# The first block's scores placed in the feed-forward banks, with the front of the schedule planned again

## The chip, the cores and the metric

The kernel runs on one core of a Trainium2 chip. The metric is the device time of one execution in microseconds (us); a time quoted below is the median of several executions. PE is TensorE, ACT is ScalarE, DVE is VectorE, POOL is GpSimd, SP is SyncE. A "trace" is the record of one profiled execution.

## The reference, cut to what matters

Attention with eight global keys and a local window of 96, for 4 sequences of 768 tokens with 8 heads of 64; then a feed-forward layer with softplus over all 3072 tokens. Inputs and output are float32.

```python
scores = scale * np.matmul(q, k.transpose(0, 1, 3, 2))      # 4 x 8 x 768 x 768
keep = is_global | is_local                                 # 8 global keys, 96 local ones
scores = np.where(keep, scores - slopes * dist, -1e9)
a = softmax(scores)
x = np.matmul(a, v) ...                                     # -> 3072 x 512
h = x @ w_in                                                # 512 -> 2048
g = np.maximum(h, 0) + np.log1p(np.exp(-np.abs(h)))         # softplus
return g @ w_out                                            # 2048 -> 512
```

## The kernel before

The tokens are cut into 24 blocks of 128 (attention) and 12 groups of 256 (feed-forward). A block needs only the keys of itself and of the block before it. A built-in list scheduler orders all operations of all engines; each operation is given with a rank and an estimated duration, and some 200 hand-tuned constants (`NUDGE`) push single operations forward or back. So a program is a layout plus a set of constants that were tuned for this layout.

The pieces of PSUM that matter: two score tiles `s_ps` of two banks each, two feed-forward banks `h_ps`, one bank `o_ps` and one bank `x_ps`. A block's scores are 8 heads times 128 (first block of a sequence) or 256 (other blocks) columns. They are written in one or two groups of matmuls:

```python
def scores(n, parts, rank):                     # parts: (0, 1) at once where n is in WHOLE
    ...
    def seed():                                 # only for blocks in PE_BIAS
        for part in parts:
            for y in range(2):
                src = (biasA if i else bias0)[:, part, ...]
                nc.tensor.matmul(s_ps[s_of(n, part)][:, y, 0 : 256 * u_all], ident[:], src...,
                                 start=True, stop=False, skip_group_check=True)
    ...
    def fn():
        for part in parts:
            for m in range(2):
                for u in range(u_all):
                    for y in range(2):
                        rows = slice(64 * y, 64 * y + 64)       # 64 rows of the array: one head
                        nc.tensor.matmul(reg, kt[rows, 2 * part + m, :], qv(rows, 2 * part + m),
                                         start=not biased, stop=True, skip_group_check=biased)
```

`soften()` then adds the bias on DVE (into a float32 tile `z`) where PE did not seed it, and ACT takes the exponential into `pb`; `pv()` multiplies by the values. A feed-forward slot is `mm1` (eight matmuls of 256 columns from `w_in` into an `h_ps` bank), an `Exp` and, for two slots together, a `Ln` on ACT (softplus), and later `mm2` (matmuls of 512 columns with `w_out`). In the first 33 us, where data is still being loaded, PE is kept busy with matmuls on zeros that nobody reads:

```python
def filler(j):
    def fn():
        nc.tensor.matmul(x_ps[:, 0:256], blank[:, 0:P], blank[:, 0:256])
    return op(f"fill{j}", "PE", 0.11, 1e6 + j, fn, reads=["blank"])
...
FILLERS = 90
PE_BIAS = (0, 1, 3)
WHOLE = (0, 4, 6, 7, 8, 9, 10, 12, 13, 14, 15, 16, 17, 18, 23)
...
order = pl.run()
for o in order:
    o.ins = o.fn()                              # emission in the planned order
```

The softmax here doesn't subtract the row's maximum and nothing guards it: scores larger than these inputs give would overflow.

Of the kernel before, what the change touches and what calls it, by code (L numbers as in the profile page):

```python
# [23 lines left out]
class Planner:  # L24
# [54 lines left out]
    def run(self, first=0.7, dma_first=1.0, dma_last=1.4, fixed=None, stretch=None):  # L79
# [40 lines left out]
        while True:  # L120
# [50 lines left out]
            while events and events[0][0] <= now + 1e-9:  # L171
                _, _, kind, o = heapq.heappop(events)
                if kind == "free":
                    free[o.eng] = True
                    if o.work:
                        queues[o.eng].append([o, o.work * stretch(o), now + dma_first])
                    else:
                        o.end = now
                        tell([u for u in o.users if u.eng == o.eng])
                        push(now + o.lat, "done", o)  # L180
                else:
                    o.done = True
                    tell([u for u in o.users if o.work or u.eng != o.eng])
# [6 lines left out]
FIRST_LOADS = "v0 k0 q0 i3 i1 q1 o0 v1 k1 i0 i2 i7 i4 o1 i6 q2 k2 i5 o5 o2 o3 o7 v2 o6 o4".split()  # L190
LOAD_LEAD = 2.5
LEADS = {3: 2.25, 4: 2.75, 5: 3, 6: 2.75, 7: 2.75, 8: 3.5, 9: 2.25, 10: 2.75, 11: 3.5}
FILLERS = 90
TABLE_RANK = -9000.0
BIAS0_ON = ["ACT", "DVE"]
BIASA_ON = ["ACT"]
PE_BIAS = (0, 1, 3)
PE_KEYS = {
    0: (("s", 1, 0), ("s", 1, 1), ("h1",), ("o",)),
    1: (("s", 0, 0), ("s", 0, 1), ("s", 1, 0), ("s", 1, 1)),  # L200
    2: (("s", 1, 0), ("x",), ("s", 0, 0), ("s", 0, 1)),
}
PE_X = {0: ("h0",), 1: ("h0",), 2: ("o",), 3: ("o",), 4: ("x",), 5: ("x",)}
# [11 lines left out]
    (0, 0): ("s", 0, 0),  # L215
# [7 lines left out]
NARROW = (0,)  # L223
TAIL = 8.0
ENG = {
    0: {"k": ["POOL", "DVE"], "q": ["POOL", "ACT"], "tk": ["DVE", "ACT"], "tq": ["DVE", "DVE"], "v": ["POOL"]},
    1: {"k": ["DVE", "POOL"], "q": ["POOL", "DVE"], "tk": ["ACT", "DVE"], "tq": ["DVE", "DVE"], "v": ["POOL", "DVE"]},
    2: {"k": ["ACT", "DVE"], "q": ["POOL", "POOL"], "tk": ["DVE", "DVE"], "tq": ["DVE", "DVE"], "v": ["POOL", "ACT"]},
}
ENG_X = {0: "DVE", 1: "ACT", 2: "DVE", 3: "DVE", 4: "ACT", 5: "ACT"}  # L230
ENG_W = {
    "i0": "DVE",
    "i1": "POOL",
    "i2": "POOL",
    "i3": "DVE",
# [5 lines left out]
    "o1": "POOL",  # L241
# [10 lines left out]
    "a0.2": 2,  # L252
    "a0.5": 1,
    "a0.6": -1,
    "a0.7": 0.5,
    "a1.0": -2,
    "a1.1": -1,
    "a1.3": -2,
    "a1.4": -2,
    "a1.5": 4,  # L260
    "a1.6": 2,
# [4 lines left out]
    "b0.0.10": 0.5,  # L266
    "b0.0.14": 0.5,
    "b0.0.4": 0.5,
    "b0.0.6": -8,
    "b0.0.8": -1,  # L270
    "b0.1.0": 1,
    "b0.1.10": 1,
    "b0.1.12": 1,
    "b0.1.2": -8,
    "b0.1.8": -8,
    "b1.0.0": -0.5,
    "b1.0.10": -0.5,
    "b1.0.12": 1,
    "b1.0.14": 4,
    "b1.0.2": -1,  # L280
    "b1.0.6": -1,
# [6 lines left out]
    "biasFalse0": -1,  # L288
    "biasFalse1": -2,
    "biasFalse2": 0.5,  # L290
    "biasFalse3": -2,
    "biasFalse4": -2,
    "biasFalse5": 4,
    "biasFalse6": -4,
    "biasFalse7": -2,
    "biasTrue0": 1,
    "biasTrue1": -4,
    "biasTrue3": 2,
    "biasTrue4": 4,
    "biasTrue6": 0.5,  # L300
    "biasTrue7": 2,
    "castk0.1": -8,
    "castk1.0": 1,
    "castk1.1": 4,
    "castk2.0": 8,
    "castk2.1": 1,
    "castk3.00": -0.5,
    "castk3.10": -0.5,
    "castk4.00": 8,
    "castk4.01": -8,  # L310
    "castk4.11": 8,
    "castq0.0": 1,
    "castq0.1": 0.5,
    "castq1.1": -1,
    "castq2.0": -4,
    "castq2.1": 8,
    "castq4.0": 8,
    "castv0.00": -4,
    "castv0.11": -0.5,
    "castv1.00": -8,  # L320
    "castv1.01": 2,
    "castv1.11": -2,
    "castv2.00": 0.5,
    "castv2.01": -0.5,
    "castv2.10": 8,
    "castv2.11": -8,
    "castv3.11": -2,
# [5 lines left out]
    "cin2": -1,  # L333
    "cin3": 4,
    "cin4": -2,
    "cout0": -2,
    "cout1": 1,
    "cout3": -0.5,
    "cout5": -1,
    "cout6": -4,  # L340
    "cpk0.0": -1,
    "cpk0.1": 2,
    "cpk1.0": 0.5,
# [4 lines left out]
    "cpq2.0": 0.5,  # L348
    "cpq2.1": 8,
    "d0": 0.5,  # L350
    "d0e": 2,
    "dl0a": 2,
    "dl0b": 0.5,
    "dl0c": 8,
    "dl1a": 8,
    "dl1c": 8,
    "e0.1": 4,
    "e0.3": 2,
    "e0.5": 1,
    "e0.7": -8,  # L360
    "e1.0": -8,
    "e1.2": 8,
    "e1.4": -8,
    "e1.5": -1,
    "e1.6": -4,
    "e1.7": 4,
# [4 lines left out]
    "ex1.1": -1,  # L371
    "ex2.0": -2,
    "ex3.1": 8,
    "ex4.1": -1,
    "ex5.0": -0.5,
    "ex5.1": 1,
    "gk5": -8,
    "gk7": 0.5,
    "gv4.0": -0.5,
    "gv4.1": 8,  # L380
    "gv5.0": 1,
    "gv5.1": 2,
    "gv6.0": -8,
    "gv6.1": 4,
    "gv7.0": 2,
    "gv8.0": -8,
    "gv8.1": -0.5,
    "ldk0.0": 1,
    "ldk0.1": -1,
    "ldk1.0": 8,  # L390
    "ldk1.1": -0.5,
    "ldk2.0": 2,
    "ldk4": 8,
    "ldk5": 0.5,
    "ldq0.0": -0.5,
    "ldq0.1": 8,
    "ldq1.0": 2,
    "ldq2.0": 0.5,
    "ldq2.1": 2,
    "ldq3": -4,  # L400
    "ldv1": 8,
    "ldv2": 8,
# [4 lines left out]
    "ln0.0": -1,  # L407
    "ln0.1": 1,
    "ln0.3": -2,
    "ln1.0": 2,  # L410
    "ln1.1": 0.5,
    "ln1.3": -4,
    "nm0.0": -0.5,
    "nm0.1": -1,
    "nm1.0": -0.5,
    "nm2.1": -1,
    "nm3.0": 0.5,
    "nm4.0": 0.5,
    "nm4.1": -0.5,
    "nm5.0": -4,  # L420
    "nm5.1": 8,
    "nm6.0": 2,
    "nm6.1": 1,
    "oc0.0.0": 8,
    "oc0.1.0": -0.5,
    "oc1.0.0": 2,
    "ones": 4,
    "pv0.1": -8,
    "pv1.0": -8,
    "pv1.1": -1,  # L430
    "pv2.0": -2,
    "pv3.0": -1,
    "pv4.1": 8,
# [4 lines left out]
    "sb1.0": 1,  # L438
    "sb1.1": -0.5,
    "sb2.0": -2,  # L440
    "sb3.0": -2,
    "sb4.0": 1,
    "sb4.1": -4,
    "sc0.1": -4,
    "sc1.0": 8,
    "sc1.1": 0.5,
    "sc2.0": -0.5,
    "sc3.0": -8,
    "sc4.0": -0.5,
    "sc5.1": -1,  # L450
    "sc6.1": -4,
    "sc7.0": -0.5,
    "sc7.1": 4,
    "st0.0.0": 0.5,
    "st0.1.0": -1,
    "st1.0.0": -4,
    "table": -1,
    "trk0.0": -8,
    "trk2.0": 0.5,
    "trk2.1": 2,  # L460
    "trk3": 0.5,
    "trk4": -2,
    "trq0.0": -4,
    "trq1.0": -0.5,
    "trq1.1": -2,
    "trq2.0": 2,
    "trq3": -0.5,
    "trq4": 8,
    "win0": 8,
    "win1": 8,  # L470
    "win2": -1,
    "win3": -2,
    "win4": -2,
    "win5": 8,
    "win6": 0.5,
    "win7": -8,
    "wout0": 1,
    "wout3": -1,
    "wout4": 4,
    "wout5": 4,  # L480
    "wout6": 0.5,
    "wout7": 8,
    "xc0": 2,
    "xc1": 8,
    "xc2": -1,
    "xc3": -2,
    "xc4": -1,
    "xc5": -4,
    "xt1": -1,
    "xt2": 1,  # L490
    "xt3": 2,
    "xt4": 1,
    "xt5": 0.5,
    "z4.0": 1,
    "z4.1": 0.5,
# [4 lines left out]
DIST0_ON = "ACT"  # L500
S_ON = {
    (0, 0): 0,
    (0, 1): 1,
    (1, 0): 0,
    (1, 1): 1,
# [5 lines left out]
    (4, 1): 1,  # L511
# [3 lines left out]
    (6, 1): 1,  # L515
    (7, 0): 1,
    (7, 1): 0,
}
T0 = 11.0
LATER = 55.0  # L520
MARGIN = {-1: 10.5, 0: -15.0, 1: 69.0, 2: 65.5, 3: 21.0}
SOONER = {"cin": -20.0, "cout": -25.0}
LAST_KEYS = (("s", 0, 0), ("x",), ("o",))
WHOLE = (0, 4, 6, 7, 8, 9, 10, 12, 13, 14, 15, 16, 17, 18, 23)
LOAD_ON = {"q0": "ACT"}


@with_exitstack
def kernel(
# [11 lines left out]
    nc = tc.nc  # L541
# [110 lines left out]
    def raw_slot(name):  # L652
        raw_of[name] = len(raw_of) % NRAW
        return raw_of[name]
# [38 lines left out]
    def load_w(which, p, rank, eng):  # L693

        slot = raw_slot((which, p))
        half, c = p % 2, p // 2
        raw = raw_t[slot][:].rearrange("p (a c) -> p a c", a=2)
        cost, issue = (1.37, 86.0), 0.45
        if which == "in" and c in NARROW:
            raw = raw_t[slot][:].rearrange("p (a c) -> p a c", a=NM)  # L700
            src = moe_w_in[:, W * p : W * p + W]
            dst = w_in_bf[:, :, W * p : W * p + W]
            cost, issue = (1.51, 51.0), 1.05
        elif which == "in":
            src = moe_w_in[W * half : W * half + W, 512 * c : 512 * c + 512]
            dst = w_in_bf[:, 2 * half : 2 * half + 2, 512 * c : 512 * c + 512]
        else:
            src = moe_w_out[W * p : W * p + W, :]
            dst = w_out_bf[:, 2 * p : 2 * p + 2, :]
        op(f"w{which}{p}", "SP", issue, rank, lambda: nc.sync.dma_start(raw, src.rearrange("(a p) c -> p a c", p=P)),  # L710
           writes=raw_keys(slot), dma=cost)
        op(f"c{which}{p}", eng, t_copy(eng, 1024, True), rank, lambda: copy_on[eng](dst, raw),  # L712
           reads=raw_keys(slot), writes=[("w" + which, p)], port=eng == "DVE")
# [71 lines left out]
    def kt_of(n):  # L785
        return kt_unit(unit_of(n))[:, n % 2, :, :]
# [13 lines left out]
    def v_keys(n):  # L800
        return [("vb", vb_slot(n), r) for r in range(2)]
# [71 lines left out]

    def scores(n, parts, rank):
# [70 lines left out]
    def pv(n, part, key, rank):  # L945
        i = blocks[n][1]
        u_all = 2 if i else 1
        pb, xs = pb_t[(2 * n + part) % NPB], xs_t[n % NXS]
# [4 lines left out]
        def mm():  # L953
            for h in range(4):
                for u in range(u_all):
                    nc.tensor.matmul(  # L956
                        xv[:, h, :], pb[:, u_all * (2 * (h % 2) + h // 2) + u, :],
                        vb_of(prev if u else n)[:, 4 * part + h, :], start=u == 0, stop=u == u_all - 1,
                    )

        reads = [("pb", (2 * n + part) % NPB), "ones"] + v_keys(n) + (v_keys(prev) if i else [])
# [232 lines left out]
    def attend(n, rank):  # L1194
# [4 lines left out]
        for parts in ((0, 1),) if n in WHOLE else ((0,), (1,)):  # L1199
            scores(n, parts, rank + 0.1 * parts[0])  # L1200
            for part in parts:
                soften(n, part, rank + 0.1 * part)
# [137 lines left out]
```

## Time and profile before

| | before |
|---|---|
| median time | 222.69 us (222.26 to 223.04, 3 runs) |
| span in the trace | 219.9 us |
| PE / ACT / DVE / POOL busy | 97% / 73% / 50% / 42% |
| matmuls, of which fillers | 2062, 90 |

The page divides the span into 40 slices of 5.5 us; a digit is the busy share of a slice in tenths. These are the three rows that the argument uses:

```profile
PE   8999999999999999999999999999999999999994
...
ACT  5664979936889798678788688678689678887300
...
DMA  5999999999999797999993241999921222011112
```

PE is at 9 in every slice between the first and the last. In the front ACT reaches 9 in slices 5, 7 and 8, and the DMA engines are nearly full for the first half. A 9 for PE says nothing about what PE does: in slices 1 to 6 a large part are fillers.

### The profile page before, as it was taken

The page shows a single profiled execution, that of the slowest core. Times are in us where ns is not written, and L with a number is a line of the kernel's source. Part 1 is how long each engine was busy: PE and PEld are TensorE (multiplying, and loading weights), DVE is VectorE, ACT ScalarE, POOL GpSimd, SP SyncE. Part 2 cuts the span into 40 slices and gives each one's busy share as a digit, 9 for nine tenths or more (in the row PEclk, how much of TensorE's full clock was granted, in tenths as well). Part 3 has the DMA queues.
Part 4 walks back from the last instruction along what each step waited for, and adds up shares of the span by engine and source line. Part 5 has one row for each costly group of instructions (what it writes and reads, how often), then busy time and mean ns, then how long its engine had stood idle before and what let it go on. Part 6 is the DMA issues. An engine that isn't in the chain of part 4 may idle for free.

```text
span 219.9 us, 5042 instructions
## 1 busy us (share of the span) xinstructions
PE 213.5 (97%) x2034; PEld 150.1 (68%) x2062; DVE 109.5 (50%) x204; ACT 160.1 (73%) x216; POOL 91.6 (42%) x156
## 2 busy tenths in 40 slices
PE   8999999999999999999999999999999999999994
PEld 6787786656685876666757757766657777767554
DVE  6467465644676567338347348347548642001121
ACT  5664979936889798678788688678689678887300
POOL 4647776787551566804972403126702220000000
DMA  5999999999999797999993241999921222011112
GB/s 207 329 351 377 380 362 381 290 254 232 241 236 256 232 235 180 190 272 243 174 205 84 51 143 60 141 263 303 162 81 51 51 72 72 3 48 48 44 56 95
DMA packets 70359, 40.96 MB, mean 186 GB/s; under 512 B 30144, under 2 KB 62272, under 8 KB 70336
## 3 DMA queue, kind: packets, MB, share of 16 engines
q1 hardware_dynamic: 69904, 40.05, 71.9%
q10 hardware_dynamic: 432, 0.59, 0.8%
q8 instruction: 16, 0.26, 0.5%
q14 instruction: 7, 0.06, 0.1%
HBM read 27.26 MB, written 6.29 MB: 153 GB/s over the span
## 4 chain that ended last, share of the span: by engine, by line
PE 82%; DMA 10%; ACT 3%; SPq 3%; issue 1%; DVE 0%; ACTq 0%
PE h_ps L1013 35%; PE o_ps L1062 30%; PE s_ps L1062 5%; PE s_ps L906 5%; PE x_ps L956 5%; DMA raw<-in_moe_w_in_dram 4%; DMA raw<-in_k_dram 4%; DMA raw<-in_v_dram 2%; PE x_ps L1062 2%; SPq L710 2%; ACT e L1028 1%; ACT g L1039 1%; SPq L675 1%; ACT vb L754 1%; ACT kb L730 0%
## 5 line engine op out<-in xcount | busy, mean ns | idle before, releaser
L1013 PE MATMUL h_ps<-XT,w_in_bf 128*128 128x256 bf16 x768 | 95.9, 273 | 0.8 <-ACT e L1028 0.5
L1013 PEld LDWEIGHTS <-w_in_bf 128*128 128x128 bf16 x768 | 72.7, 98 | 18.1 <-issue 0.6
L1028 ACT ACTIVATE e<-h_ps 128x512 f32<-128x512 f32 x96 | 60.1, 631 | 31.6 <-PE h_ps L1013 31.3
L1062 PE MATMUL o_ps<-w_out_bf,g 128*128 128x512 bf16 (+1 forms) x296 | 74.1, 371 | 1.2
L1062 PEld LDWEIGHTS <-g 128*128 128x128 bf16 x416 | 37.5, 98 | 29.3
L932 DVE TENSOR_TENSOR z<-s_ps,biasA 128x1024 f32<-128x1024 f32 x36 | 43.3, 1219 | 17.9 <-PE s_ps L906 12.8
L1039 ACT ACTIVATE g<-e 128x1024 bf16<-128x1024 f32 x48 | 50.7, 1057 | 1.4
L939 ACT ACTIVATE pb<-z 128x1024 bf16<-128x1024 f32 (+1 forms) x42 | 41.1, 987 | 4.1 <-DVE z L932 4.0
L754 POOL CAST vb<-raw 64x512 bf16<-64x512 f32 x44 | 27.5, 624 | 14.9 <-DMA raw<-in_v_dram 13.2
L754 POOL CAST kb<-raw 64x512 bf16<-64x512 f32 x36 | 22.3, 620 | 25.9 <-DMA raw<-in_k_dram 24.6
L1091 DVE COPY osb<-o_ps 128x512 f32<-128x512 f32 (+1 forms) x20 | 13.4, 670 | 38.2 <-PE o_ps L1062 38.0
L863 POOL COPY vb<-vb 4x512 bf16<-4x512 bf16 x32 | 19.9, 621 | 29.6 <-PE x_ps L956 26.3
L956 PEld LDWEIGHTS <-pb 128*128 128x128 bf16 x352 | 16.6, 98 | 5.8
L966 DVE RECIPROCAL rcp<-x_ps 128x4 f32<-128x4 f32 x40 | 7.1, 179 | 23.5 <-PE x_ps L956 23.4
L967 DVE TENSOR_TENSOR xs<-x_ps,rcp 128x256 bf16<-128x256 f32 x40 | 17.0, 424 | 1.4
L956 PE MATMUL x_ps<-vb,pb 128*128 128x65 bf16 x304 | 15.9, 193 | 0.0
L1174 PE MATMUL x_ps<-blank 128*128 128x256 bf16 x90 | 12.9, 295 | 1.1 <-DVE blank L1113 1.1
L1062 PE MATMUL s_ps<-w_out_bf,g 128*128 128x512 bf16 (+1 forms) x62 | 13.1, 352 | 0.1
L906 PEld LDWEIGHTS <-kT 64*128 64x128 bf16 x224 | 6.8, 94 | 6.1 <-issue 5.7
L1174 PEld LDWEIGHTS <-blank 128*128 128x128 bf16 x90 | 9.0, 107 | 2.9 <-DVE blank L1113 1.0
L906 PE MATMUL s_ps<-qT,kT 64*128 64x128 bf16 x224 | 10.5, 218 | 0.0
L712 POOL CAST w_out_bf<-raw 128x1024 bf16<-128x1024 f32 x7 | 7.3, 1039 | 3.4 <-DMA raw<-in_moe_w_out_dram 3.4
(72 smaller groups left out, 102.9 us busy)
## 6 DMA issues: line engine op xcount, KB each, us to landing
raw<-in_v_dram SPq DMA_DIRECT2D x12, 512.0 KB, 5.2
out_dram<-osb SPq DMA_DIRECT2D x23, 256.0 KB, 2.8
raw<-in_q_dram SPq DMA_DIRECT2D x9, 512.0 KB, 5.4
raw<-in_k_dram SPq DMA_DIRECT2D x9, 512.0 KB, 5.8
raw<-in_moe_w_in_dram SPq DMA_DIRECT2D x8, 512.0 KB, 9.9
raw<-in_moe_w_out_dram SPq DMA_DIRECT2D x8, 512.0 KB, 9.3
raw<-in_k_dram SPq DMA_DIRECT2D x6, 256.0 KB, 6.2
raw<-in_q_dram SPq DMA_DIRECT2D x4, 256.0 KB, 8.1
```

The lines of the kernel that those rows point to most:

```text
L754: copy_on[eng](dst, src)
L863: nc.gpsimd.tensor_copy(vb_of(prev)[sl, :, 0:D], vb_of(first)[sl, :, 0:D])
L906: nc.tensor.matmul(reg if unit_of(n) in WIDE else reg.rearrange("p (r t) -> p r t", r=2), kt[rows, 2 * part + m, :], qv(rows, 2 * part + m ...
L932: nc.vector.tensor_tensor(z, src, bias, ALU.add)
L939: nc.scalar.activation(pb[:, 0:nr, :].rearrange("p (y a) b -> p y (a b)", y=2), src, AF.Exp, scale=1.0 / root_d)
L956: nc.tensor.matmul(xv[:, h, :], pb[:, u_all * (2 * (h % 2) + h // 2) + u, :], vb_of(prev if u else n)[:, 4 * part + h, :], start=u == 0, s ...
L967: nc.vector.tensor_tensor(xs[:, 4 * part : 4 * part + 4, :], xv[:, :, 0:D], rcp[:][:, :, None].to_broadcast([P, 4, D]), ALU.mult,)
L1013: last = nc.tensor.matmul(hv[:, j, :], w_in_bf[:, m, fb * P : fb * P + P], XT[g % NXG][:, m, :], start=(m == 0), stop=(m == NM - 1),)
L1028: nc.scalar.activation(e[:, p % 2, :, :].rearrange("p j (b t r) -> p (j b) r t", b=2, r=2), hb[:].rearrange("p (a r t) -> p a r t", a=4, r=2),
L1039: nc.scalar.activation(gt[:, 2 * p - 2 : 2 * p + 2, :].rearrange("p a t -> p (a t)"), e[:].rearrange("p a j t -> p (a j t)"), AF.Ln, bias=1.0,
L1062: nc.tensor.matmul(bank(key)[:, 0 : z - a], gt[:, fb, ns * P : ns * P + P], w_out_bf[:, fb, a:z], start=(fb == 0), stop=(fb == NFB - 1),)
L1174: nc.tensor.matmul(x_ps[:, 0:256], blank[:, 0:P], blank[:, 0:256])
```

## The change

Intent: the first block and the second block both wanted the two score tiles. The first block's eight heads (eight times 128 columns) now go into the two feed-forward banks, which are free at that time, even heads in one and odd heads in the other. The second block has the score tiles to itself. The plan of the front was tuned anew for that. The core of the diff:

```diff
+    def scores_lone(n, rank):
+        qv, kt = q_of(n), kt_of(n)
+        keys = [("h0",), ("h1",)]
+        def seed():
+            for part in range(2):
+                for y in range(2):
+                    nc.tensor.matmul(
+                        h_ps[y][:, 256 * part : 256 * part + 256], ident[:],
+                        bias0[:, part, 2 * y : 2 * y + 2, :].rearrange("p a b -> p (a b)"),
+                        start=not part, stop=False, skip_group_check=True,
+                    )
+        def fn():
+            for a in range(4):
+                for y in range(2):
+                    reg = h_ps[y][:, P * a : P * a + P]
+                    nc.tensor.matmul(... kt[64 * y : 64 * y + 64, a, :], qv(slice(64 * y, 64 * y + 64), a),
+                                     start=False, stop=True, skip_group_check=True)
+        ...                                     # two exponentials of 128x512, one from each bank, into one pb
...
-        for parts in ((0, 1),) if n in WHOLE else ((0,), (1,)):
+        if n in LONE:
+            scores_lone(n, rank)
+        for parts in () if n in LONE else ((0, 1),) if n in WHOLE else ((0,), (1,)):
...
+LONE = (0,)
-PE_BIAS = (0, 1, 3)
+PE_BIAS = (0, 1)
-NARROW = (0,)
+NARROW = ()
-WHOLE = (0, 4, 6, 7, 8, 9, 10, 12, 13, 14, 15, 16, 17, 18, 23)
+WHOLE = (0, 2, 4, 6, 7, 8, 9, 10, 11, 12, 13, 14, 15, 16, 17, 18, 21, 22, 23)
-FIRST_LOADS = "v0 k0 q0 i3 i1 q1 o0 v1 k1 i0 i2 i7 i4 o1 i6 q2 k2 i5 o5 o2 o3 o7 v2 o6 o4".split()
+FIRST_LOADS = "k0 q0 v0 i3 i1 q1 k1 o0 i0 i2 i4 v1 i6 o1 i7 q2 k2 i5 o4 o5 o2 o3 o6 o7 v2".split()
...                                             # engines of casts and copies, some 200 NUDGE constants,
...                                             # leads and margins of the planner; FILLERS stays 90
```

## The prediction

> **What bounds the kernel now.** I read the page's busy table first, then its chain of waits, then TensorE's own waits, then the timeline of the first 36 us.
>
> ```profile
> PE 213.5 (97%) x2034; PEld 150.1 (68%) x2062; DVE 109.5 (50%) x204; ACT 160.1 (73%) x216; POOL 91.6 (42%) x156
> ...
> PE 82%; DMA 10%; ACT 3%; SPq 3%; issue 1%; DVE 0%; ACTq 0%
> ```
>
> PE is 97% busy and carries 82% of the chain that ends last. A busy PE may still be waiting inside modelled matmul ends, so I checked its waits and, from starts to starts, its rate.
>
> ```profile
> PE x_ps L1174 <- DVE blank L1113: 1.1, 1, 1.1
> PE h_ps L1013 <- ACT e L1028: 0.5, 2, 0.2
> PE h_ps L1013 <- POOL w_in_bf L712: 0.3, 1, 0.3
> PE s_ps L815 <- ACT qb L730: 0.2, 1, 0.2
> ```
>
> These are all the waits of the whole run: 1.1 us before the first instruction and 1.0 us later, none after 36 us. From 40 us on, a slot of eight first-layer matmuls takes 0.87 us and eight second-layer matmuls 1.73 us in the chain; gaps of 0.22 us occur only behind groups of three or seven second-layer matmuls, which is one matmul record missing (2034 of 2062 are in the trace), not a wait. So the kernel is one packed PE stream. What is not useful in it is 90 filler matmuls (L1174, which multiply zeros) in the first 33 us, the 1.05 us start, and about 2.8 us between the last matmul and the end. A change of order pays only by taking matmuls or waits out of that stream.
>
> ```profile
> 9.94 0.60 PE L887 MATMUL s_ps<-bias,ident 128*128 128x256 bf16 x4
> 10.47 0.40 PE L906 MATMUL s_ps<-qT,kTa 64*128 64x128 bf16 x8
> 10.80 1.26 PE L1174 MATMUL x_ps<-blank 128*128 128x256 bf16 x10
> ...
> 12.25 0.81 PE L887 MATMUL s_ps<-biasA,ident 128*128 128x512 bf16 x3
> 12.99 0.62 PE L906 MATMUL s_ps<-qT,kTa 64*128 64x128 bf16 x16
> ...
> 20.49 0.60 PE L887 MATMUL s_ps<-biasA,ident 128*128 128x512 bf16 x2
> ...
> 21.49 1.99 PE L1013 MATMUL h_ps<-XT,w_in_bf 128*128 128x256 bf16 x16
> ```
>
> This is PE's timeline in the front. Block 0's scores end at 10.8, block 1's only at 13.5: it needs the same two score tiles, so its bias seeding waits until the two exponentials of block 0 (10.80 to 11.89 on ACT) have emptied them. Ten fillers stand in that hole. The first feed-forward matmul (L1013) runs at 21.49.
>
> **What the Trainium skill says.** "TensorE: Matmul & The Clock Gate", section "Wait — 56ns, not 53.3ns?": warm matmuls start N/2.4 GHz + 2.5 ns apart, so 109 ns at 256 columns and 216 ns at 512. The trace agrees: 0.87/8 = 109 ns and 1.73/8 = 216 ns. Nothing is left to gain in the rate. "PSUM — Partial Sum Buffer", section "The four PSUM rules": a bank holds 512 fp32 columns, and of several groups in it only the first matmul may carry the clearing flag. That is why the new block 0 (four heads of 128 columns per bank) starts only its first seed of each bank; the trace of before cannot show it. "DMA: Bandwidth & Descriptors", section "Issuing engines are not separate DMA queues": all issuers share 16 engines. So an earlier place in the load order is paid by what moves back. The trace agrees: full engines (DMA share 1.06 at 10 to 20 us), and the fourth weight load of the first layer, issued at 11.94, landed at 21.27.
>
> **The change, part by part.**
> 1. Block 0 goes to the two feed-forward banks. The same 4 seeds of 256 columns, 8 score matmuls and two exponentials of 128x512 remain; block 1 gets its banks at once. By the order of the built program, block 1's 16 score matmuls follow three fillers, two fillers and one, instead of ten. With the measured durations: query and key transposes start behind 38 fillers at about 6.7 and end at 8.3; the key copy (1.01 us on ACT, free at 8.5) ends near 9.6; block 0 scores at about 10.0, block 1 at 10.8 to 11.3 instead of 13.5. Two microseconds earlier on block 1, but PE time is not removed: fillers stay 90, 85 of them before the first L1013 in both programs. They move to later holes.
> 2. Block 3 loses its PE bias: four 512-column matmuls. Two take 20.49 to 20.93 = 0.44 us, so four take **0.87 us off PE**. In exchange DVE gets two additions of 1.22 us (row L932). DVE is 50% busy; with its reads before 24 us they end ahead of the exponential that ACT takes then. Off the path.
> 3. More blocks are scored whole: 28 score groups with block 0's, against 31. In the chain a group of 8 takes 0.33 us and one of 16 takes 0.55, so each merge saves 0.11: 3 x 0.11 = **0.33 us**.
> 4. Casts move among engines: ACT takes four casts of v rows (4 x 0.62) and all biases, GpSimd all eight first-layer weights; GpSimd drops ten row casts. In 0 to 22 us ACT's work rises from about 14 to 17.7 us (counts times durations). It still fits before the first feed-forward exponential.
> 5. The first-layer weights i0 and i1 become wide. Before, the half that is cast at 16.3 served a slot alone; now slots 0 and 1 need both i1 and i0. On GpSimd the order is i3, i1, v copy, i6, v copy, i0.
>
> ```profile
> 18.46 1.04 POOL L712 CAST w_in_bf<-raw 128x1024 bf16<-128x1024 f32 x1 [1.12 <-DMA raw<-in_moe_w_in_dram]
> 19.45 1.27 POOL L863 COPY vb<-vb 4x512 bf16<-4x512 bf16 x2
> ...
> 21.29 1.08 DVE L712 CAST w_in_bf<-raw 128x1024 bf16<-128x1024 f32 x1 [1.18 <-DMA raw<-in_moe_w_in_dram]
> ```
>
> The load at ninth place (512 KB each, counting from the start) lands at 18.46 and the eleventh at 21.29: 1.4 us each. In the new order i6 is ninth and i0 tenth, so i0 lands near 19.9. GpSimd casts i6 from 18.46 to 19.5, copies v rows (0.63) to 20.1, casts i0 to 21.15; with 0.15 us for the signal the first L1013 can start at **21.3**.
>
> When would PE get there? It ran L1013 at 21.49; less 0.87 (seeds), less 0.2 (wait for the query cast, absorbed) and less about 0.25 (other order of fillers and seeds): 20.2. So a new wait of about 1.1 us on GpSimd's cast of i0 appears, and of 1.3 us gained, 0.2 is left at 21.3. From there to the end of block 4's scores before took 12.2 us (21.49 to 33.66), while its pieces add up to about 10.9 (eight slots 7.0, two transposes 1.7, value products, fillers and scores 2.2). About 1.3 us of wait and hand-over lie in it. In the new order I find only one likely wait: the third query's transposes come at about 26.8, but its casts move to DVE (two of 0.45, from a landing near 26.4), so 27.5: 0.7. That leaves 0.6 us gained. From 33 to 37 us before waits 0.5 on the exponentials; I count 0.2 for after.
>
> Sum: 0.2 + 0.6 + 0.3 + 0.33 (merged groups, later) = **about 1.4 to 1.5 us**. The end of the program (80 second-layer matmuls in the same four groups) is the same instruction for instruction, so its 2.8 us stays. 222.69 - 1.5 = **221.2 us**.
>
> **Rivals.**
> A. The front pays fully: i0 is there when PE arrives and no query wait comes. Then all 1.2 us of PE work and nearly the 1.0 us of waits and some hand-over go: 220.0. For it: the order of fillers was chosen for a start near 20. Against: the landing rate of 1.4 us per load and GpSimd's queue, full of 1.04 us casts.
> B. The new waits take the place of all that was removed, and ACT, already full from 35 to 40 us (5.00 of 5), slips with more casts early: 222.5 to 223. For it: PE waits in no place now, so a small slip of any feeder is paid. Against: the ACT rows from the first feed-forward exponential on are nearly the same set in both programs.
> C. The second half of the run gets new holes from the changed leads and fused scores (two banks are released together, exponentials later). DVE and ACT are busy for 27.5 and 38.9 of the 50 us from 100 to 150; I give it 0.3 us at most.
> D. The 2.2 us that block 1 wins counts in full. I reject this: with 90 fillers in both programs and PE in order, early data only changes what stands idle.
>
> **Range and chances.** The floor is the stream without removable waits, 222.69 - 1.2 - 1.0 - 0.6 of hand-over = 219.9; run-to-run spread is 0.4. The other side is rival B. Range **219.7 to 222.7**, centre **221.2**. Faster than 218.2 would need four more microseconds of PE work gone, which nothing here removes: 0.03. Slower than 227.1 needs a broken feeder for 4 us: 0.02. Within 2%: 0.95.
>
> **What would show it.** PE matmuls: 8 seeds in place of 12, with 90 fillers still. Block 1's scores near 11 us: part 1. First L1013-like matmul near 21.3, its wait released by GpSimd's w_in cast: part 5; if it starts by 20.3 without one, rival A. A wait on the DVE query cast near 27: the 0.7. No PE wait after 45 us: against C. If the time is outside the range, a wait of over 2 us stands in PE's waits, or the fillers' time shrank.

## The result, and the profile after

| | before | after |
|---|---|---|
| median time | 222.47 us (222.08 to 223.04, 4 runs) | 219.73 us (219.26 to 220.23, 4 runs) |
| ratio | | 0.9875, 95% interval 0.9842 to 0.9908 |
| span in the first trace | 219.9 us | 218.3 us |

A ratio here is the mean time of one kernel's runs over that of the other's runs of the same rounds, so it is not quite the ratio of the medians beside it. Executions over 1.5% slower than the fastest of the same kernel are left out of the means. The change is worth 1.25% (0.9 to 1.6%), or 2.7 us as a difference of medians. The prediction was 221.2 us and a gain of 1.5 us; 219.73 lies at the lower edge of its range of 219.7 to 222.7.

The busy table and the by-engine shares of the chain of waits, after:

```profile
PE 212.2 (97%) x2028; PEld 150.7 (69%) x2058; DVE 111.7 (51%) x203; ACT 163.1 (75%) x223; POOL 90.0 (41%) x153
...
PE 88%; DMA 4%; SPq 4%; issue 1%; POOL 1%; DVE 0%; POOLq 0%
```

The four seeds are gone (2062 weight loads became 2058), nothing else left PE, and the share of DMA and ACT in the chain fell from 13% to 4%. PE's own waits in the same trace, with their length in us, how often, and the longest:

```profile
PE x_ps L1226 <- DVE blank L1165: 1.1, 1, 1.1
PE h_ps L1065 <- POOL w_in_bf L722: 0.4, 1, 0.4
PE o_ps L1114 <- issue: 0.3, 2, 0.2
```

Against three kinds of waits after the start before, two remain, and one of them ("issue") waits for nothing that the profile shows. PE's timeline of the front (start, length, what; in brackets the idle time ahead of it and its cause):

```profile
11.16 0.40 PE L902 MATMUL h_ps<-qT,kTa 64*128 64x128 bf16 x8
11.49 0.60 PE L936 MATMUL s_ps<-biasA,ident 128*128 128x512 bf16 x2
12.03 0.62 PE L955 MATMUL s_ps<-qT,kTa 64*128 64x128 bf16 x16
...
21.96 1.92 PE L1065 MATMUL h_ps<-XT,w_in_bf 128*128 128x256 bf16 x16 [0.36 <-POOL w_in_bf L722]
...
26.60 1.04 PE L1065 MATMUL h_ps<-XT,w_in_bf 128*128 128x256 bf16 x8
27.52 1.05 PE L825 MATMUL s_ps<-ident,qb 128*128 128x128 bf16 x8
```

The second block's 16 score matmuls (L955) start at 12.03 instead of 12.99, with the first block's (L902) just ahead of them in the other banks. The first feed-forward matmul (L1065) starts at 21.96, later than the 21.49 before, so the front up to this point won nothing in this trace. The third query's transposes (L825 at 27.52) follow the slot ahead of them without a wait.

Behind it, the feed-forward slot after block 4's scores starts at 33.02 (before: 33.68). The chain of waits of the kernel before, in order of time (start, length, what), shows a gate that the prediction passed over: it read only the chain's shares and PE's waits.

```profile
21.29 8.08 DMA raw<-in_k_dram
...
29.47 0.62 ACT kb L730
...
31.72 0.62 ACT vb L754
32.35 0.62 ACT vb L754
32.99 1.16 ACT e L1028 x2
34.18 1.06 ACT g L1039
35.23 0.53 ACT e L1028
35.81 1.03 PE h_ps L1013 x8
```

The chain runs from the landing of the third unit's keys at 29.4 through a packed row of ACT work to the feed-forward slot at 35.81, and only then does PE carry it. The wait itself shows as 0.22 us, which looks small; but the time at which this slot starts is set by ACT, not by PE. After, the chain leaves the loads much earlier:

```profile
10.36 9.79 DMA raw<-in_moe_w_in_dram
20.19 0.62 POOL vb L873
20.86 1.05 POOL w_in_bf L722
21.96 1.92 PE h_ps L1065 x16
```

From 21.96 to the end it is PE alone. The changed kernel casts the key half at 28.57 instead of 29.47, and the two value casts that ACT did at 31.72 for 1.25 us are on DVE and POOL.

### The profile page after: what moved, and what is told of

The parts are those of the page before. It is cut to its first block, busy times and chain, and to the rows that moved or that the text cites. A ratio compares the mean times of both kernels' runs of the same rounds, so it can differ in the third digit from the quotient of the medians.

```text
span 218.3 us, 5040 instructions
## 1 busy us (share of the span) xinstructions
PE 212.2 (97%) x2028; PEld 150.7 (69%) x2058; DVE 111.7 (51%) x203; ACT 163.1 (75%) x223; POOL 90.0 (41%) x153
## 4 chain that ended last, share of the span: by engine, by line
PE 88%; DMA 4%; SPq 4%; issue 1%; POOL 1%; DVE 0%; POOLq 0%
PE h_ps L1065 39%; PE o_ps L1114 30%; PE s_ps L1114 5%; PE s_ps L955 5%; PE x_ps L1007 5%; DMA raw<-in_moe_w_in_dram 4%; PE x_ps L1114 2%; SPq L679 2%; SPq L720 2%; PE s_ps L825 1%; SPq L689 1%; POOL w_in_bf L722 0%; POOL vb L873 0%; PE o_ps L1007 0%; PE x_ps L1038 0%
## 5 line engine op out<-in xcount | busy, mean ns | idle before, releaser
L1065 PE MATMUL h_ps<-XT,w_in_bf 128*128 128x256 bf16 x768 | 95.7, 273 | 0.5 <-POOL w_in_bf L722 0.4
L1065 PEld LDWEIGHTS <-w_in_bf 128*128 128x128 bf16 x768 | 73.0, 98 | 17.7 <-POOL w_in_bf L722 0.6
L1114 PE MATMUL o_ps<-w_out_bf,g 128*128 128x512 bf16 (+1 forms) x293 | 73.3, 371 | 1.6 <-issue 0.3
L988 ACT ACTIVATE pb<-z 128x1024 bf16<-128x1024 f32 (+1 forms) x44 | 43.2, 988 | 9.8 <-DVE z L981 9.6
L981 DVE TENSOR_TENSOR z<-s_ps,biasA 128x1024 f32<-128x1024 f32 x38 | 45.5, 1217 | 8.3 <-PE s_ps L955 4.1
L764 POOL CAST vb<-raw 64x512 bf16<-64x512 f32 x40 | 24.6, 614 | 16.7 <-DMA raw<-in_v_dram 15.1
L1226 PE MATMUL x_ps<-blank 128*128 128x256 bf16 x90 | 14.7, 314 | 1.1 <-DVE blank L1165 1.1
L1226 PEld LDWEIGHTS <-blank 128*128 128x128 bf16 x90 | 9.5, 113 | 3.6 <-DVE blank L1165 1.1
L722 POOL CAST w_in_bf<-raw 128x1024 bf16<-128x1024 f32 x8 | 8.3, 1038 | 5.0 <-DMA raw<-in_moe_w_in_dram 4.9
L955 PEld LDWEIGHTS <-kT 64*128 64x128 bf16 x224 | 6.8, 94 | 4.9 <-issue 4.4
L955 PE MATMUL s_ps<-qT,kT 64*128 64x128 bf16 x224 | 10.0, 218 | 0.0
```

The source lines that it names most:

```text
L764: copy_on[eng](dst, src)
L955: nc.tensor.matmul(reg if unit_of(n) in WIDE else reg.rearrange("p (r t) -> p r t", r=2), kt[rows, 2 * part + m, :], qv(rows, 2 * part + m ...
L981: nc.vector.tensor_tensor(z, src, bias, ALU.add)
L988: nc.scalar.activation(pb[:, 0:nr, :].rearrange("p (y a) b -> p y (a b)", y=2), src, AF.Exp, scale=1.0 / root_d)
L1065: last = nc.tensor.matmul(hv[:, j, :], w_in_bf[:, m, fb * P : fb * P + P], XT[g % NXG][:, m, :], start=(m == 0), stop=(m == NM - 1),)
L1114: nc.tensor.matmul(bank(key)[:, 0 : z - a], gt[:, fb, ns * P : ns * P + P], w_out_bf[:, fb, a:z], start=(fb == 0), stop=(fb == NFB - 1),)
```

## The experiments

Fifteen runs were made, in four jobs; each job is compared with runs of the kernel before on the same chip (medians 222.37, 222.40, 222.40 and 222.64; the second and the third job, on one chip, share eleven of these). The unaltered changed kernel was run in the first and the last job only, so in the other two a difference to it goes across jobs. Line numbers in these traces shift by a few where an edit added lines.

### 1. Both kernels unaltered, again

No edit. The question was whether the length of PE's slow phase at the start decides the time, since the traces before and after differ there: in the first trace before, 14 fillers of 256 columns started 213 ns apart until the rate became 109 ns, in the trace after 25 (26 in the text below; this is a recount).

> The changed kernel unaltered, timed again in five rounds, to get the size of the gain apart from luck. In the two traces so far the ends differ by 1.6 us (219.9 and 218.3), the medians by 2.7. The trace of before had 14 slow filler matmuls (213 ns apart instead of 109) at its start, the trace of after 26; 12 x 0.104 = 1.25 us. Theory C (cold start luck): the true gain is near 2.7 us and this profile has fewer slow fillers than 26 or again a time above its median. Theory U (unlucky sample of four): the true gain is the 1.5 us that was worked out, 221.0 against 222.5.

> The kernel before unaltered, one look, for a second trace of its start. Theory C: the number of slow fillers differs from 14, and the first feed-forward matmul moves with it by 0.104 us for each. Theory U: 14 again.

The changed kernel took 219.69 us (6 runs, ratio 0.9879, 0.9853 to 0.9906), the one before 222.57 in one look. Both had 16 slow fillers this time, and the gap stayed. So the slow phase is a scatter of both kernels, not the cause. A third set of runs in the last job gave the same:

> The changed kernel unaltered once more, on the same chip as the two runs beside it, to compare them without the spread of the kernel before. 219.6 if the earlier runs hold.

219.89 us (ratio 0.9887, 0.9858 to 0.9915). The trace of these runs had 19 slow fillers, its first feed-forward matmul at 20.77, and no wait of PE at all after the start; its span was 217.1. One and the same kernel reached the end of its matmuls at 215.2, 215.4 and 214.0 in three traces. What moved with it were the loads: GpSimd's cast of i1, which the traces show released by its load, began at 17.55, 17.13 and 15.69, and that of i0, which opens the feed-forward, at 20.86, 20.45 and 19.38.

### 2. The named part alone, and everything but the named part

The changed kernel with the first block back in the score tiles, and the kernel before with the new place of the first block and all its old constants. The scheduler plans both again.

```diff
-LONE = (0,)
+LONE = ()                     # a_nolone, on the changed kernel
```
```diff
+LONE = (0,)                   # b_lone, on the kernel before, with scores_lone() and the new pv()
```

> The changed kernel with block 0 back in the score banks (the named part of the change undone, the rest of its constants kept, the planner lays out the order anew). Theory L (block 0's own banks carry the gain): back to 222 or above. Theory O (the gain is PE work and waits removed by the new order and constants): 219.5 to 221.

> The kernel before with only block 0 moved into the feed-forward banks (all other constants as before, order laid out anew). Theory L: faster than before by 1 us or more, to 221.5 or below. Theory O: no gain, 222.5 to 224, as block 1 is scored sooner but 90 fillers and the seeds of block 3 stay.

Neither is a gain. Without the new place the changed kernel took 223.34 us (ratio to before 1.0029, 0.9998 to 1.0060); the new place with the old constants took 225.28 (median of five runs of six; 1.0141, 1.0100 to 1.0181). PE's waits in the trace of the latter show why the second says little of the layout itself:

```profile
PE h_ps L1063 <- DMA XT<-xs: 1.6, 1, 1.6
...
PE s_ps L823 <- POOL qb L738: 0.7, 1, 0.7
```

The old constants, tuned for another layout, leave a transpose through DMA in front of a feed-forward slot. In these two versions neither layout nor constants paid alone; as the order was planned anew in both, they do not price either by itself.

### 3. Does PE work in the front count in full?

Two tests of the same four seeds. In the changed kernel four dummy matmuls of 512 columns were added ahead of block 3's scores, which then overwrite them. In the kernel before, block 3's seeds were not issued, so its bias is missing (a wrong result). The order of all else was kept.

```diff
+            if n == 3:                                     # a_pad3, on the changed kernel
+                for part in parts:
+                    for y in range(2):
+                        nc.tensor.matmul(s_ps[s_of(n, part)][:, y, :], ident[:], biasA[:, part, ...])
```
```diff
-            for part in parts:                             # b_noseed, on the kernel before
+            for part in parts if n != 3 else ():
-                                start=not biased, ...
+                                start=not biased or n == 3, ...
```

> The changed kernel, order kept, with four matmuls of 512 columns put back before block 3's scores (their result is overwritten): the PE time of the four seeds that the change took out. Theory P (the PE stream counts in full, so the seeds were worth their 4 x 0.216): 0.86 us slower than the changed kernel, 220.5. Theory F (the front waits for loads and casts until the first feed-forward matmul, so PE work taken out before it was worth little): within 0.4 us, 219.7 to 220.1.

> The kernel before, order kept, without the four seeding matmuls of block 3 (wrong result for that block on purpose): the same term in the other kernel. Theory P: 0.86 us faster than before, 221.5. Theory F: the first feed-forward matmul has its data by 20.1 in this kernel, so here too the loads hold only what follows; under F less than 0.4 us faster, 222.0 or more.

Putting four matmuls in cost the changed kernel 0.7 to 0.9 us: 220.57 (ratio 0.9914, 0.9890 to 0.9939) against medians of 219.69 to 219.89 for the unaltered one in other jobs. Their PE time is 4 x 0.216 = 0.86, and no new wait stands in the trace. Taking the same four out of the kernel before won about 0.3 us: 222.06 against 222.40, ratio 0.9988 (0.9963 to 1.0013, so between 0.8 won and 0.3 lost). PE's waits of that trace:

```profile
PE h_ps L1013 <- ACT e L1028: 0.6, 2, 0.4
PE o_ps L956 <- ACT pb L939: 0.5, 1, 0.5
```

Most of what was taken out came back as waits on ACT: 0.5 us on an exponential of the scores, which did not stand there before, and the longest wait on the feed-forward exponentials grew from 0.2 to 0.4. The 0.5 stands at 21.12, where the seeds were, before block 2's value products: its scores, their addition on DVE and their exponentials on ACT take longer than PE now does to get there. By the medians the same term has two prices: in the kernel before, what follows swallows more than half of it, in the changed kernel it counts in full. The intervals are wide and touch, so it is the new waits, read in one trace, that make this reading more than a guess.

### 4. Is it one gate?

If the row of ACT work at 29 to 36 us were the only gate of the kernel before, freeing ACT there would pay, alone or together with the missing seeds. Two value casts were moved from ACT to GpSimd, and one weight cast from GpSimd to DVE so that GpSimd had room; PE's order was kept.

```diff
-op(f"c{which}{p}", eng, ..., lambda: copy_on[eng](dst, raw), ...)
+op(f"c{which}{p}", eng, ..., lambda: copy_on["DVE" if (which, p) == ("in", 4) else eng](dst, raw), ...)
+                if which == "v" and i == 2 and eng == "ACT":
+                    def fn(dst=dst, src=src):
+                        nc.gpsimd.tensor_copy(dst, src)
...
+    moved = next(o for o in order if o.name == "cin4")      # to DVE's queue, behind xc2
+    order.remove(moved)
+    order.insert(next(j for j, o in enumerate(order) if o.name == "xc2") + 1, moved)
```

> The kernel before, PE order kept, with two feeders changed: the two casts of v rows that ACT did at 31.7 to 33.0 go to GpSimd, and the last first-layer weight cast (i4) goes from GpSimd to DVE. In its traces PE waited 0.3 us on that cast and 0.5 us on ACT's exponentials. Theory W (these waits are part of what the changed kernel gained after its first feed-forward matmul): 0.5 to 0.8 us faster than before, near 221.7. Theory N (another wait takes their place): within 0.2 us of before.

> The same, and the four seeding matmuls of block 3 left out as well (wrong result for that block on purpose). Theory W: with the feeders sooner the seeds' 0.86 us pay too, 1.3 to 1.7 us faster than before, near 221.0. Theory N: as without the feeders' change, 0.3 us faster, 222.1.

Nothing: 222.42 (1.0006, 0.9974 to 1.0038), and 222.17 with the seeds away as well (0.9991, 0.9966 to 1.0016). In the trace of the first the waits on the feed-forward exponentials were gone, as wanted. But in that execution PE waited 1.5 us, up to 8.24, for a cast of the first keys, and the traced execution of the second had 28 slow fillers, so their fronts can't be compared with the others'; the timed runs alone carry the verdict. So it is not one gate: with ACT relieved, the time does not fall. In the trace of the second, PE's longest wait on data after the start is again the 0.55 us on block 2's exponentials, at 21.95: in both traces without seeds this part of their 0.86 is lost ahead of the first feed-forward matmul, whatever ACT does later. A smaller one, 0.3 us near 75 us for GpSimd's copies of value rows, stands also in the traces of `b_noseed` and `b_again`. Neither stands in the three traces of the changed kernel. No run removes them, so that they hold the kernel before is not shown.

### 5. What a group of score matmuls costs at its edges

The score matmuls use 64 rows of the array, all others 128. The prediction counted 0.11 us per group from the chain of waits of the kernel before. These rows of that view show what it read and what it missed:

```profile
96.61 0.33 PE s_ps L906 x8
96.94 0.97 PE o_ps L1062 x4
97.91 0.87 PE h_ps L1013 x8
98.78 0.86 PE o_ps L1062 x4
99.64 0.55 PE s_ps L906 x16
```

Eight score matmuls take 0.33 us and sixteen take 0.55: eight cost 0.22 and the group 0.11 on top. That was counted. The row behind it was not: four second-layer matmuls take 0.97 us behind a score group and 0.86 elsewhere. The edge is paid on both sides. From the start of one matmul to that of the next, I get 0.096 us extra on entering and 0.121 on leaving, 0.22 us per group.

To measure it by time, a dummy matmul of 8 columns on the full array was put between the two halves of 15 whole groups of the changed kernel:

```diff
+                if i and part and len(parts) == 2:          # a_split, on the changed kernel
+                    nc.tensor.matmul(s_ps[s_of(n, part)][:, 0, 0:8], ident[:], ident[:, 0:8])
```

> The changed kernel, order kept, with one matmul of 8 columns over all 128 rows between the two halves of each of the 15 whole blocks of 16 score matmuls: this measures what one more score group costs. The prediction's term (0.11 us for leaving a group, plus 0.025 for the small matmul): 15 x 0.135 = 2.0 us slower. Theory H (entering costs as well: in the traces the step into a group is 0.096 longer and the step out of it 0.121): 15 x 0.24 = 3.6 us slower.

222.60 us, ratio to before 1.0009 (0.9983 to 1.0035): 2.9 us more than the unaltered kernel's 219.69, or 0.19 for each of the 15. The chain of this trace shows one of them:

```profile
52.17 0.33 PE s_ps L957 x8
52.50 0.11 PE s_ps L949
52.62 0.33 PE s_ps L957 x8
52.95 0.98 PE h_ps L1067 x8
```

L949 is the dummy. From 52.17 to 52.95 it is 0.78 us, where an unsplit group of sixteen takes 0.55. The result lies between the two theories (2.0 and 3.6): the entry costs too, but in time not all of the steps count. Three groups fewer are worth 0.65 us by the steps in the traces and at most 0.6 by this run (3 x 0.19, dummy included), not 0.33.

### 6. Are the fillers dead weight?

The last 16 of the 90 fillers (1.75 us of PE time) were not issued, the order of the rest kept.

```diff
+        if o.name.startswith("fill") and int(o.name[4:]) >= 74:     # a_skip16
+            continue
```

> The changed kernel, order kept, without its last 16 filler matmuls (11 before the first feed-forward matmul, 5 after it). Theory D (fillers are dead weight in the stream): 16 x 0.109 = 1.75 us faster than the changed kernel, 218.0. Theory G (in this kernel the front is gated by the cast of the weights i0, which ends at 21.5 to 21.9, and by the exponentials): the fillers turn into waits, at most 0.4 us faster, 219.3 or above.

219.64 us (0.9893, 0.9862 to 0.9924), no gain. In its trace the first feed-forward matmul starts at 20.86, as early as in the best trace of the unaltered kernel, and behind it stand waits that were not there:

```profile
PE h_ps L1065 <- ACT e L1080: 0.7, 1, 0.7
...
PE o_ps L1007 <- ACT pb L988: 0.3, 1, 0.3
```

So the fillers stand where PE would wait anyway: real data arrives at its own time. I combined this with an exchange of two weight loads and a further `z` buffer, to see whether a version beats both kernels:

```diff
-    z_t = ring("z", NZ, [P, 8, P], F32)
+    z_t = ring("z", NZ + 1, [P, 8, P], F32)             # the extra one for block 3, part 1
+    swap("win6", "win0")                                # a_best: load and cast of i0 ahead of i6
+    swap("cin6", "cin0")
+    order = [o for o in order if not (o.name.startswith("fill") and int(o.name[4:]) >= 74)]
```

> An attempt to beat both kernels: the changed kernel, PE order kept, with the weights i0 loaded and cast before i6, a fourth buffer for block 3's biased scores (its addition waited 0.7 us for one), and without the last 16 fillers, which alone gained nothing. Theory G (three gates, each hidden behind the other): 0.5 us faster than the changed kernel, 219.2. Theory X (exponentials and loads hold the front anyway): within 0.2 us of it, 219.5 to 219.9.

219.84 us (0.9885, 0.9862 to 0.9908): the first feed-forward matmul came at 20.06, and the time is that of the changed kernel. PE's timeline in this trace shows where much of the head start went: into a wait for the third query's cast on DVE, which the prediction had named.

```profile
26.40 1.05 PE L825 MATMUL s_ps<-ident,qb 128*128 128x128 bf16 x8 [1.08 <-DVE qb L740]
```

No version here beats the changed kernel.

### 7. What the earlier second block is worth

The name of the change promises an earlier second block. Nine fillers and the second block's seeding were moved behind the first block's scores, with the same matmuls in all; the aim was that its scores end near 13.5 us, as they did before.

```diff
+    late = [names[f"fill{j}"] for j in range(44, 53)] + [names["sb1.0"]]    # a_late1, a_late1b
+    order = [o for o in order if o not in late]
+    at = order.index(names["sc0.0"]) + 1
+    order[at:at] = late
```
```diff
+    late = [names[f"fill{j}"] for j in range(44, 62)] + [names["sb1.0"]]    # a_late2: nine fillers more
```

> The changed kernel with block 1's seeds and scores held back on PE behind nine fillers that stood later, so that they end near 13.5 us, as in the kernel before; block 0 keeps its own banks. Theory E (scoring block 1 sooner is what the named part of the change pays with): 1 us or more slower than the changed kernel, 220.7 or above. Theory D (the rejected rival of the prediction turned round: early scores only change what stands idle): within 0.3 us of the changed kernel, 219.4 to 220.0.

> The kernel with block 1 held back by nine fillers, again, beside the changed kernel on one chip: its times were 0.7 us above the changed kernel's, its one trace no later. Theory E: 0.5 to 0.9 us slower than the changed kernel again, with a wait of PE on block 1's exponentials before the second unit's transposes. Theory D: within 0.3 us of it.

> The changed kernel with block 1's scores held back by 18 later fillers instead of nine, so that they end about 1 us later than in the kernel before; all other orders kept. Theory E (block 1's scores lead a chain that PE waits for: its exponentials free the bank that the second unit's transposes need): about 1 us slower still than with nine, 221.2 or above. Theory D (only idle time changes): as with nine, 220.4 or below.

The first try cost 0.7 us (220.40; 0.9903, 0.9877 to 0.9930) against the unaltered kernel of the first job, the repeat was 0.4 us faster than the unaltered kernel of its own job (219.52; 0.9872, 0.9849 to 0.9896). Nothing is settled for nine fillers. They are also only half of the delay: the scores start at 12.76 and 13.34 in these traces, but with 22 and 28 slow fillers. Less 0.104 us for each above 14, that is 11.9 in both, where the kernel before has 12.99 (14 slow ones) and the changed kernel 11.05 (16). With eighteen they start at 13.24 with 14 slow ones, 0.25 us later than before and not 1 us. That run is the one that undoes the advance. It took 220.88 us (0.9929, 0.9903 to 0.9955), 1.0 us more than the unaltered kernel of its job and between the figures of the two theories (single executions overlap: 220.31 to 221.21 against 219.17 to 221.00). Its trace has waits on the second block's exponentials:

```profile
PE s_ps L825 <- ACT pb L988: 0.6, 1, 0.6
...
PE h_ps L1007 <- ACT pb L988: 0.3, 1, 0.3
```

So in the changed kernel's order about 1 us of the second block's 2 us seems to be needed, and the rest is slack. This is no share of the gain: the order of the kernel before has no such waits with its second block that late.

### Where the time went

To add it up, I took the starts of all matmuls in two traces of the kernel before and three of the changed one, all unaltered, and subtracted the time each matmul takes at the full rate in these traces. What is left is time between matmuls. The table gives its mean (us) in four stretches:

| stretch | before | after | gain |
|---|---|---|---|
| start to the first feed-forward matmul, slow fillers included | 3.06 | 3.86 | -0.80 |
| from there to 34 us | 1.66 | 0.56 | 1.10 |
| 34 to 60 us | 1.37 | 0.97 | 0.40 |
| after 60 us | 4.83 | 4.05 | 0.78 |
| the four seeds, taken out | | | 0.86 |

The sum is 2.3 us, and the last matmul starts at 217.2 before and 214.9 after in these traces. The executions that were traced took 221.98 and 222.57 us before, 220.23, 220.43 and 219.17 after; their means differ by 2.3 as well. So the table accounts for the traced executions in full. The medians of all runs differ by 2.7; two of the three traced executions of the changed kernel were the slowest of their series. The 0.4 us between can't be placed, having no trace. The first row holds the slow fillers, which were few (14 and 16) in the two traces of before and more (25, 16, 19) in those of after: on the mean 5 more, some 0.5 us of the 0.8.

What the second and third rows gained can be named from the same starts. In the first trace before, four steps of PE are longer than the matmul ahead of them (and, at 33.68, the edge of a score group) takes: 0.49 us at 26.47 (a weight cast on GpSimd), 0.23 at 27.58 (the third query's cast on GpSimd, not among the waits that the prediction read), 0.31 at 33.68 and 0.39 at 35.81 (feed-forward exponentials), 1.4 in all. The second trace before has the same four, 1.5 in all. In the traces after, none of them stands; the one large step in their place is 0.52 us in the second trace, at 29.66, for the attention output that DVE scales (`xs`).

## Why the prediction was right or wrong

**Right, the mechanism.** PE is one packed stream, and only matmuls and waits taken out of it count. There are still 90 fillers and 8 seeds in place of 12. Past the first 36 us no wait on another engine's data appears in the three traces of the changed kernel, which speaks against rival C. The end is unchanged. Rival D, that the two microseconds of the second block count in full, falls by experiment 7, but so does the reason given against it, that early data only changes what stands idle: in the changed order about half of them seems to be needed. Block 1's scores, forecast at 10.8 to 11.3, ended at 12.58, 11.60 and 11.92 in the three traces. Rival B, new waits in place of all that was removed, did not come: after the start PE's waits list 0.7, 1.0 and 0.0 us in the three traces, against 1.0 in the first before.

**Right, part 2.** The four seeds were put at 0.87 us of PE time, and in the changed kernel four such matmuls cost 0.7 to 0.9 of run time. But the forecast took this as a property of the term. In the kernel before, the same four are worth about 0.3. I read this as gates that the other parts of the change moved: block 2's exponentials close behind the seeds (0.55 us in both traces without seeds) and the row of ACT work later. The traces of both kernels fit that, and no run isolates it.

**Right in the main, part 5.** The first feed-forward matmul was put at 21.3, released by GpSimd's cast of i0. It came at 21.96, 21.54 and 20.77 in three traces. In the first the wait and its releaser are the ones named, 0.36 us instead of the forecast 1.1; in the other two PE's waits list none there. PE itself came where the forecast had it: the 20.77 of the third trace, less 0.52 us for its five more slow fillers than the first trace before had, is 20.25 (an estimate), against 20.2. The forecast treated a landing time as fixed that scatters by more than a microsecond. Its 0.15 us for the signal was a guess; here PE starts 0.05 us behind the cast's end.

**Wrong in size, the step "I find only one likely wait ... 0.7. That leaves 0.6 us gained."** The wait did not come. The third query's transposes start at 27.52, 27.14 and 26.28 in the three traces, each time straight behind the slot ahead of them, and DVE's cast ended at 27.47, 27.09 and 26.13, just in time. It was there in hiding: where PE was earlier, in the last version of experiment 6, PE waited 1.08 us for it. In the first trace the forecast's time of 27.5 came true, but PE was itself not there earlier, as its first feed-forward slot had come 0.66 late: two late feeders don't add up, the later one counts. To the feed-forward slot behind block 4's scores the forecast had a gain of 0.8 in all. Against the mean of the two traces before (33.68 and 34.00), the three after (33.02, 33.18 and 31.76) gained 0.8, 0.7 and 2.1. So the forecast held in two traces, and where the loads landed early neither of its two waits existed and the gain was over twice as large. On the mean it is 1.2. Two mistakes stand behind it: the landing times of one trace were taken as fixed, and of the 1.4 us of steps that stood in the kernel before (behind the table's second and third rows) 0.7 was expected to come back as the query wait and 0.2 to stay. All of it went, and in two of the three traces nothing took its place.

**Wrong in size, part 3.** "Each merge saves 0.11: 3 x 0.11 = 0.33." A merge saves 0.22 by the steps in the traces (at most 0.19 by the time of experiment 5), since the group's edge is paid on entering and on leaving; three are 0.65 by the first price, all of them lie after 60 us, and that stretch gained 0.78. The missing half was in the row behind the group, in a view that the forecast had open.

**Close, two small terms.** For the front up to the first feed-forward matmul the forecast had 0.2 of gain; the seeds' 0.86 less the lost 0.80 gives 0.06. For 33 to 37 us it had 0.3, and 34 to 60 us gained 0.4. ACT's work in the first 22 us, which it put at 14 and 17.7 us by counts, is 12.7 and 16.0 in the traces; the rise, and that it fits, was right.

**What was overlooked without entering the sum.** The chain of waits of before runs over ACT until 35.81, which the shares "DMA 10%; ACT 3%" announced. Read in order of time it would have shown that in this trace, as in the second, the front of the kernel before is gated by the third unit's keys, and that any PE saving ahead of it has to be tested against it. It is not the only gate, since experiment 4 relieved this row and won nothing.

In sum: 0.06 + 1.1 + 0.4 + 0.78 = 2.3 us in the traces, where the forecast had 0.2 + 0.6 + 0.3 + 0.33 = 1.4. The two mis-sized terms, 0.6 against 1.1 and 0.33 against 0.78, make up nearly all of the difference. Rival A, "the front pays fully: 220.0", was nearer than the centre: the third trace comes close to it (no wait, though the start is 20.77 and not by 20.3), and the merged groups come on top.

**Open.** What part of the gain belongs to the first block's own banks: both tests of it were planned again by a scheduler whose constants fit another layout. And that gates stand one behind another in the kernel before is what experiments 3 and 4 together suggest (taking away the seeds, ACT's casts or both pays about 0.3 us by the medians, with intervals that include zero). The traces show two candidates for what holds once ACT is relieved, block 2's exponentials (0.55 us) and GpSimd's value copies near 75 us (0.3), but no run took either away.

## What to carry to other kernels

A saving on the bounding engine pays only up to the next gate behind it, so test a term in the kernel where it will live: the same four matmuls were worth 0.7 to 0.9 us in one program and, by the medians, about 0.3 in the other. And take a landing time from several traces, not from one. Read the chain of waits in order of time, not only by its shares, since a wait of 0.2 us may be all that shows of an engine that sets the time. When you price a hand-over, compare the row ahead and the row behind with the same rows elsewhere; a cost read on one side alone was half of what the steps add up to.

## What the Trainium skill lacked or had wrong

- "TensorEngine Tiling (Array Packing)", section "Key Properties", says that changing the tiling mode drains TensorE. It gives no price. The traces fit that, and the price here is 0.096 us on entering a group of 64-row matmuls and 0.121 on leaving it; 15 forced changes and returns, each with one 8-column matmul, cost 2.9 us of time, 0.19 each.
- "TensorE: Matmul & The Clock Gate", section "What's actually happening", puts the slow phase at some 3.4 us and says that the count of slow matmuls varies from run to run. The variation agrees, but the phase was often longer: over the 17 traces 14 to 28 fillers of 256 columns started 213 ns apart at the beginning, 3.0 to 6.0 us. The profile's clock row, on the pages that have one, reads 9 already in the first slice.
- No page that I read says how far the landing of one load scatters between executions of a kernel. Here, in three traces of one kernel, the cast of i1 that waits for its load began at 17.55, 17.13 and 15.69 us, and the first feed-forward matmul came at 21.96, 21.54 and 20.77.
